# Grouping attention steps around column-tiled output products, with three more crossbar transposes, in a fused retention and feed-forward kernel

## Chip, cores, metric

One core of one Trainium2 chip. The metric is device microseconds of one execution; medians of several runs are quoted. A run over 1.5% above the fastest of its kernel counts as slow and is left out of ratios wherever enough fast runs are there. A ratio is the mean time of one kernel's fast runs over that of the other's of the same rounds, so it is not quite the ratio of the medians quoted beside it.

## The reference

```
q, k, v: (8, 8, 576, 64) float32        # batch, heads, sequence, head dim
gamma[h] = 1 - 2 ** (-5 - h)
scores   = (q @ k.T) / 8 * gamma ** (i - j) for i >= j, else 0
x = (scores @ v), heads side by side    # (4608 tokens, 512)
h = x @ w_in                            # (4608, 2048)
out = (h * sigmoid(beta * h)) @ w_out   # (4608, 512)
```

## The kernel before

The sequence is cut into chunks of 128 rows (the fifth of each batch has 64), 40 in all, and retention is linear: a chunk needs its own masked scores and a running state. Per chunk: prepare (scale queries, cast keys, scale values), transpose queries and keys, scores, mask, output = masked scores x values + queries x state, update the state. The result lands in `xT`, which feeds projections in blocks of 512 tokens: 16 `up` groups of four products, then 16 `down` groups of four. Attention of the next block is interleaved with the projections of this one: each step has a position counted in groups.

```python
NV = 3
vpads = [consts.tile([P, H, P], BF16, name=f"vpad{i}") for i in range(NV)]   # values, zero padded

def a_X(i):                     # transposes by DMA, issued from ScalarE
    ...
    nc.scalar.dma_start_transpose(qkT.rearrange("p j pr s -> p (j pr) s")[:, :, :cL],
                                  L["qk"][:cL].rearrange("p j h d -> p (j h d)"))

def a_sc(i):                    # scores: two heads side by side in half-row tiles
    ...
            nc.tensor.matmul(sc[j][:cL, p, :cL], L["kT"][r, p, :cL], L["qT"][r, p, :cL], ...)
    ...                         # two masks on VectorE

def a_O(i):
    ...
    if c > 0:                   # read the state
        for p in range(HP):
            nc.tensor.matmul(O[:, p, :cL], sbds[(i - 1) % NS][:, p, :], L["qT"][:, p, :cL], ...)
    for j in range(2):          # full-width products; the padding adds zeros for the other head
        for p in range(HP):
            nc.tensor.matmul(O[:, p, :cL], vp[:cL, 2 * p + j, :], R[:cL, j, p, :cL], ...)
    nc.vector.tensor_copy(xT[:, :, n0:n0 + cL], O[:, :, :cL])

def attn_steps(i, at, gap=2.0):
    if i < XB:                  # XB = 14: TensorE transposes
        return [(at - 4, F(pre, i)), (at - 3.9, F(load_next, i)), (at, F(a_T, i)), (at + gap, F(a_sc, i)),
                (at + 2 * gap, F(a_st, i)), (at + 2 * gap, F(a_O, i))]
    return [(at - 10, F(pre, i)), (at - 9.9, F(load_next, i)), (at - 5, F(a_X, i)), (at + gap, F(a_sc, i)),
            (at + 2 * gap, F(a_st, i)), (at + 2 * gap, F(a_O, i))]
```

So a crossbar transpose is issued at `at - 5` and its scores come at `at + 2`: seven groups of lead. A crossbar transpose is a DMA that transposes on its way; chunks before `XB` are transposed by TensorE instead. Lead is the distance from issue to use, latency the time from issue to landing.

## Time and profile before

| | before |
|---|---|
| time, median | 327.55 us (326.5 to 329.17) |
| span of the profiled run | 325.5 us |
| TensorE busy | 96% |
| first projection starts | 23.45 us |
| crossbar transposes | 26 |

In the lines of a profile PE is TensorE's products, PEld its weight loads, DVE is VectorE, ACT ScalarE (ACTq its queue, which issues DMAs), POOL GpSimd. A line of a timeline gives start and duration in us, engine, source line, operation, output<-inputs, shapes and count, and in brackets how long the engine had been idle and what ended that.

### The profile page before, as it was taken

What the parts mean: (1) busy time and instruction counts of PE and PEld (TensorE: products, weight loads), DVE (VectorE), ACT (ScalarE), POOL (GpSimd) and SP (SyncE); (2) the same over time, 40 slices, a digit from 0 to 9 for tenths busy, and PEclk for the clock granted to TensorE, in tenths of its full rate; (3) what the DMA queues carried; (4) which work ended last, traced back from release to release, by engine and by line L of the source; (5) the groups of instructions that cost most, each with busy time, mean ns of one, the idle gap of its engine ahead of it and who ended that gap; (6) DMA issues with size and microseconds to landing.
All of it is one profiled execution on the core that took longest, in us unless ns stands there. A gap on an engine that the chain in (4) does not pass through costs nothing.

```text
span 325.5 us, 5518 instructions
## 1 busy us (share of the span) xinstructions
PE 311.7 (96%) x2208; PEld 163.8 (50%) x2247; DVE 114.4 (35%) x202; ACT 141.6 (44%) x246; POOL 113.3 (35%) x132
## 2 busy tenths in 40 slices
PE   6779999999999999999999999999999999999995
PEld 2544584566555555544555555544545555544442
DVE  3685273634423244214423343224324432330011
ACT  2567881276237610760076106710662057305700
POOL 5323847974333354333333353333333430000000
PEclk9799999999999999999999999999999999999998
DMA  9999999999974999999999869656315121110011
GB/s 171 218 378 244 256 373 220 206 213 213 266 127 126 166 216 220 163 225 184 254 194 191 174 152 226 117 129 156 89 34 113 67 64 34 49 65 34 0 64 64
DMA packets 146362, 52.54 MB, mean 161 GB/s; under 512 B 137616, under 2 KB 137632, under 8 KB 146336
## 3 DMA queue, kind: packets, MB, share of 16 engines
q1 hardware_dynamic: 121920, 46.15, 63.8%
q10 hardware_dynamic: 24416, 6.04, 11.3%
q8 instruction: 17, 0.28, 0.4%
q14 instruction: 9, 0.07, 0.1%
HBM read 36.71 MB, written 9.44 MB: 142 GB/s over the span
## 4 chain that ended last, share of the span: by engine, by line
PE 91%; DVE 3%; DMA 2%; ACT 1%; issue 1%; ACTq 0%
PE po L296 38%; PE ph L284 37%; PE O L249 5%; PE sc L228 4%; PE st L266 2%; DMA qkT<-qk 2%; PE ph L152 2%; PE O L244 2%; PE T L212 2%; DVE R L232 1%; ACT qkT L216 1%; ACT sbd L272 0%; DVE xT L253 0%; DVE w_in_sb L130 0%; DVE tiny L160 0%
## 5 line engine op out<-in xcount | busy, mean ns | idle before, releaser
L284 PE MATMUL ph<-xT,w_in_sb 128*128 128x512 bf16 (+2 forms) x623 | 131.4, 357 | 2.5 <-DVE xT L253 1.6
L296 PE MATMUL po<-w_out_sb,gT 128*128 128x512 bf16 x556 | 130.2, 379 | 1.1 <-issue 0.2
L286 ACT ACTIVATE gT<-ph,beta_sb 128x512 bf16<-128x512 f32 (+2 forms) x160 | 101.9, 645 | 64.6 <-PE ph L284 48.2
L187 POOL TENSOR_TENSOR vpad<-qkvn,gv 128x512 bf16<-128x512 f32 (+1 forms) x40 | 42.0, 1051 | 135.9 <-issue 93.2
L284 PEld LDWEIGHTS <-w_in_sb 128*128 128x128 bf16 x640 | 59.1, 98 | 58.5 <-issue 1.6
L296 PEld LDWEIGHTS <-gT 128*128 128x128 bf16 x576 | 54.0, 98 | 60.6
L232 DVE TENSOR_TENSOR R<-sc,causal 128x512 bf16<-128x512 f32 (+1 forms) x80 | 47.2, 631 | 92.4 <-PE sc L228 92.2
L272 ACT CAST sbd<-st 64x256 bf16<-64x256 f32 x64 | 23.3, 364 | 77.2 <-PE st L266 76.4
L302 DVE COPY ot<-po 128x512 f32<-128x512 f32 x36 | 24.8, 691 | 66.1 <-PE po L296 63.9
L253 DVE CAST xT<-O 128x512 bf16<-128x512 f32 (+1 forms) x40 | 25.5, 637 | 38.2 <-PE O L249 38.2
L182 POOL TENSOR_TENSOR qk<-qkvn,gq 128x512 bf16<-128x512 f32 (+1 forms) x36 | 37.8, 1051 | 2.1 <-DMA qkvn<-in_q_dram 1.6
L249 PE MATMUL O<-R,vpad 128*128 128x128 bf16 (+1 forms) x320 | 23.5, 213 | 1.2 <-DVE R L232 1.2
L216 ACT COPY qkT<-T 128x1024 bf16<-128x1024 bf16 (+1 forms) x14 | 13.3, 950 | 21.8 <-PE T L212 21.7
L186 POOL CAST qk<-qkvn 128x512 bf16<-128x512 f32 (+1 forms) x36 | 21.9, 608 | 1.1 <-DMA qkvn<-in_k_dram 1.1
L249 PEld LDWEIGHTS <-vpad 128*128 128x128 bf16 (+1 forms) x320 | 18.2, 97 | 2.3 <-issue 1.8
L228 PEld LDWEIGHTS <-qkT 64*128 64x128 bf16 (+1 forms) x320 | 8.9, 98 | 17.7 <-issue 11.4
L228 PE MATMUL sc<-qkT 64*128 64x128 bf16 (+1 forms) x320 | 15.4, 217 | 0.9 <-ACT qkT L216 0.4
L266 PEld LDWEIGHTS <-qk 128*128 128x128 bf16 x128 | 9.5, 99 | 6.6 <-issue 0.2
L266 PE MATMUL st<-vpad,qk 128*128 128x128 bf16 x128 | 12.6, 222 | 0.1
L212 PE MATMUL T<-ident,qk 128*128 128x128 bf16 (+1 forms) x112 | 8.7, 224 | 3.1 <-DVE qk L182 3.0
L244 PE MATMUL O<-qkT,sbd 128*128 128x128 bf16 (+1 forms) x128 | 11.5, 212 | 0.0
L212 PEld LDWEIGHTS <-qk 128*128 128x128 bf16 (+1 forms) x112 | 7.2, 103 | 5.1 <-DVE qk L182 3.1
(38 smaller groups left out, 59.1 us busy)
## 6 DMA issues: line engine op xcount, KB each, us to landing
out_dram<-ot SPq DMA_DIRECT2D x36, 256.0 KB, 2.4
qkvn<-in_q_dram SPq DMA_DIRECT2D x32, 256.0 KB, 4.7
qkvn<-in_k_dram SPq DMA_DIRECT2D x32, 256.0 KB, 5.0
qkvn<-in_v_dram SPq DMA_DIRECT2D x32, 256.0 KB, 5.3
wt<-in_moe_w_in_dram SPq DMA_DIRECT2D x4, 1024.0 KB, 10.4
wt<-in_moe_w_out_dram SPq DMA_DIRECT2D x4, 1024.0 KB, 10.6
qkvn<-in_q_dram SPq DMA_DIRECT2D x8, 128.0 KB, 4.7
qkvn<-in_k_dram SPq DMA_DIRECT2D x8, 128.0 KB, 4.3
```

The costliest lines, as they stand in the source:

```text
L182: (nc.vector if first else nc.gpsimd).tensor_tensor(qn[:cL], t[:cL, 0], gq_b, ALU.mult)
L187: nc.gpsimd.tensor_tensor(vp4[:cL], t[:cL, 2].rearrange("p (pr two) d -> p pr two d", two=2), gv_b.rearrange("p (pr two) d -> p pr two d", ...
L228: nc.tensor.matmul(sc[j][:cL, p, :cL], L["kT"][r, p, :cL], L["qT"][r, p, :cL], start=True, stop=True, skip_group_check=True)
L232: nc.vector.tensor_tensor(R[:cL, j, :, :cL], sc[j][:cL, :, :cL], m_b, ALU.mult)
L249: nc.tensor.matmul(O[:, p, :cL], vp[:cL, 2 * p + j, :], R[:cL, j, p, :cL], start=(n == 0), stop=(j == 1), skip_group_check=True)
L253: nc.vector.tensor_copy(xT[:, :, n0:n0 + cL], O[:, :, :cL])
L266: nc.tensor.matmul(st[:, p, :], L["kn"][:cL, 2 * p:2 * p + 2, :].rearrange("p h d -> p (h d)"), L["vp4"][:cL, p], start=(c == 0 and p == 0 ...
L272: nc.scalar.copy(sbd[r, :, j * D:(j + 1) * D], st[r, :, j * D:(j + 1) * D])
L284: nc.tensor.matmul(ph[:, :tn], w_in_sb[:, ko, fo * P:(fo + 1) * P], xT[:, ko, x0:x0 + tn], start=(ko == 0), stop=(ko == KO - 1))
L286: nc.scalar.activation(gT[:, fo, t0:t0 + tn], ph[:, :tn], ACT.Silu, scale=beta_sb[:, fo:fo + 1])
L296: nc.tensor.matmul(po[:], gT[:, fo, ms * P:(ms + 1) * P], w_out_sb[:, fo, :], start=(fo == 0), stop=(fo == FO - 1))
L302: nc.vector.tensor_copy(ot, po[:])
```

## The change

The intent: spend less TensorE time per chunk by column tiles (two heads' outputs side by side), by visiting the attention less often (scores of chunk i with output and state of chunk i-1, in one cluster), and by leaving three more chunks' transposes to the crossbar; and start the projections earlier. Cut to its core:

```diff
-    XB = 14
+    XB = 11
-    NV = 3
-    vpads = [consts.tile([P, H, P], BF16, name=f"vpad{i}") for i in range(NV)]
+        vn = sb.tile([P, H, D], BF16, name="vn", tag="vn", bufs=4)
...
 def a_O(i):
-        if c > 0:  (state read first, then padded products)
+        for j, p in [(n // HP, n % HP) if i < 9 else (n % 2, n // 2) for n in range(H)]:
+            nc.tensor.matmul(O[j * D:(j + 1) * D, p, :cL], vn[:cL, 2 * p + j, :], R[:cL, j, p, :cL],
+                             start=(p == 0), stop=(c == 0), skip_group_check=True)
+        (then the state read, if c > 0)
...
+    def cluster(i, at):                       # chunks 9 and up
+            if i < XB:
+                st += [(at - 7, F(pre, i)), (at - 6.9, F(load_next, i)), (at - 3, F(a_T, i))]
+            else:
+                st += [(at - 10, F(pre, i)), (at - 9.9, F(load_next, i)), (at - 5, F(a_X, i))]
+            st += [(at, F(a_sc, i))]
+        if C0 <= i - 1 <= last:
+            st += [(at, F(a_O, i - 1)), (at, F(a_st, i - 1))]
...
 first stage, chunks 0 to 3
-    warm_up(12); betas(); pre(0); a_T(0); ...   (a_T(i + 1) ahead of a_O(i); key cast on ScalarE)
+    warm_up(3)  (float32); pre(0)
+    for i in range(4):
+        a_T(i)        # queries first, copied by ScalarE; keys copied by VectorE
+        warm_up(1, 256)
+        a_sc(i); pre(i + 1); a_st(i); a_O(i)     # key cast on VectorE
+    first quarter of w_in loaded and cast in two pieces of 256 columns
```

The transposes stay at `at - 5`, but the scores moved from `at + 2` to `at`.

More of the change, by code (lines that the diff above doesn't have):

```diff
@@ L72 @@
     nc.scalar.dma_start(beta_rows[:], moe_beta.rearrange("(fo p) -> fo p", p=P))
-    warm = consts.tile([P, MB], BF16, name="warm")
+    warm = consts.tile([P, MB], F32, name="warm")
     nc.vector.memset(warm[:], 0.0)
@@ L97 @@
                             fill=0.0, base=0, channel_multiplier=-1)
-    NV = 3
-    vpads = [consts.tile([P, H, P], BF16, name=f"vpad{i}") for i in range(NV)]
     NS = 2
     sbds = [consts.tile([P, HP, P], BF16, name=f"sbd{i}") for i in range(NS)]
-    nc.gpsimd.memset(vpads[0][:], 0.0)
     nc.vector.memset(sbds[0][:], 0.0)
-    nc.gpsimd.memset(vpads[1][:], 0.0)
     nc.vector.memset(sbds[1][:], 0.0)
@@ L115 @@
     WG = 4
-    FG = d_ff // WG
+    pieces = [(0, 256), (256, 256)] + [(f, 512) for f in range(512, d_ff, 512)]
+    NP = len(pieces)
     w_in_r = moe_w_in.rearrange("(ko ki) f -> ki ko f", ki=P)
     w_out_r = moe_w_out.rearrange("(fo fi) n -> fi fo n", fi=P)
-    wts = {}
+    wts, whole = {}, [None]
     def load_w_in(g):
-        t = stage.tile([P, KO, FG], F32, name="wt", tag="wt", bufs=4)
-        nc.sync.dma_start(t[:], w_in_r[:, :, g * FG:(g + 1) * FG])
+        f0, fn = pieces[g]
+        if f0 % 512 == 0:
+            t = stage.tile([P, KO, 512], F32, name="wt", tag="wt", bufs=4)
+            whole[0] = t
+        t = whole[0][:, :, f0 % 512:f0 % 512 + fn]
+        nc.sync.dma_start(t, w_in_r[:, :, f0:f0 + fn])
         wts[g] = t
@@ L127, in cast_w_in @@
         t = wts.pop(g)
+        f0, fn = pieces[g]
         for ko in range(KO):
             e = nc.gpsimd if ko == KO - 1 else nc.vector
-            e.tensor_copy(w_in_sb[:, ko, g * FG:(g + 1) * FG], t[:, ko])
+            e.tensor_copy(w_in_sb[:, ko, f0:f0 + fn], t[:, ko])
     def load_w_out(g):
@@ L134, in load_w_out @@
         nc.sync.dma_start(t[:], w_out_r[:, g * KO:(g + 1) * KO, :])
-        wts[WG + g] = t
+        wts[NP + g] = t
     def cast_w_out(g):
-        t = wts.pop(WG + g)
+        t = wts.pop(NP + g)
         for i in range(KO):
@@ L142, in cast_w_out @@
             e.tensor_scalar(w_out_sb[:, fo, :], t[:, i], rbeta_sb[:, fo:fo + 1], None, ALU.mult)
-    for g in range(WG):
+    for g in range(NP):
         load_w_in(g)
@@ L147, with warm_up @@
         load_chunk(b, c)
-    def warm_up(n):
+    def warm_up(n, cols=MB):
         ph = psum.tile([P, MB], F32, name="ph", tag="mm", bufs=3)
         for _ in range(n):
-            nc.tensor.matmul(ph[:], warm[:, :P], warm[:], start=True, stop=True, skip_group_check=True)
+            nc.tensor.matmul(ph[:, :cols], warm[:, :P], warm[:, :cols], start=True, stop=True,
+                             skip_group_check=True)
     def betas():
-        pb = psum.tile([P, FO], F32, name="pb", tag="T", bufs=1)
+        pb = psum.tile([P, FO], F32, name="pb", tag="mm", bufs=3)
         nc.tensor.transpose(pb[:], beta_rows[:], ident_f[:FO, :FO])
@@ L176, in pre @@
         qn, kn = qk[:, 0], qk[:, 1]
-        vp = vpads[i % NV]
-        vp4 = vp.rearrange("p (pr two) (x d) -> p pr (two x) d", two=2, x=2)[:, :, 0::3, :]
+        vn = sb.tile([P, H, D], BF16, name="vn", tag="vn", bufs=4)
         gq_b = gq[:cL, c, :].unsqueeze(2).to_broadcast([cL, H, D])
@@ L182, in pre @@
         (nc.vector if first else nc.gpsimd).tensor_tensor(qn[:cL], t[:cL, 0], gq_b, ALU.mult)
-        if first:
-            nc.scalar.copy(kn[:cL], t[:cL, 1])
-        else:
-            nc.gpsimd.tensor_copy(kn[:cL], t[:cL, 1])
-        nc.gpsimd.tensor_tensor(vp4[:cL], t[:cL, 2].rearrange("p (pr two) d -> p pr two d", two=2),
-                                gv_b.rearrange("p (pr two) d -> p pr two d", two=2), ALU.mult)
-        live[i] = dict(qk=qk, qn=qn, kn=kn, vp=vp, vp4=vp4)
+        (nc.vector if first else nc.gpsimd).tensor_copy(kn[:cL], t[:cL, 1])
+        nc.gpsimd.tensor_tensor(vn[:cL], t[:cL, 2], gv_b, ALU.mult)
+        live[i] = dict(qk=qk, qn=qn, kn=kn, vn=vn)
     def load_next(i):
@@ L209, in a_T @@
         T = psum.tile([P, 2, HP, P], BF16, name="T", tag="T", bufs=1)
-        for j, src in enumerate((L["qn"], L["kn"])):
+        T2 = psum.tile([P, 2, HP, P], BF16, name="T2", tag="mm", bufs=3) if i < 4 else T
+        qkT = sb.tile([P, 2, HP, P], BF16, name="qkT", tag="qkT", bufs=4)
+        for j, (src, t) in enumerate(((L["qn"], T), (L["kn"], T2))):
             for p in range(HP):
-                nc.tensor.transpose(T[:, j, p, :cL],
+                nc.tensor.transpose(t[:, j, p, :cL],
                                     src[:cL, 2 * p:2 * p + 2, :].rearrange("p h d -> p (h d)"),
                                     ident[:cL, :cL])
-        qkT = sb.tile([P, 2, HP, P], BF16, name="qkT", tag="qkT", bufs=4)
-        nc.scalar.copy(qkT[:, :, :, :cL], T[:, :, :, :cL])
+            if i < 4:
+                (nc.vector.tensor_copy if j else nc.scalar.copy)(qkT[:, j, :, :cL], t[:, j, :, :cL])
+        if i >= 4:
+            nc.scalar.copy(qkT[:, :, :, :cL], T[:, :, :, :cL])
         L["qT"], L["kT"] = qkT[:, 0], qkT[:, 1]
@@ L238, in a_O @@
         L = live[i]
-        R, vp = L["R"], L["vp"]
+        R, vn = L["R"], L["vn"]
         O = psum.tile([P, HP, P], F32, name="O", tag="O", bufs=1)
-        n = 0
+        for j, p in [(n // HP, n % HP) if i < 9 else (n % 2, n // 2) for n in range(H)]:
+            nc.tensor.matmul(O[j * D:(j + 1) * D, p, :cL], vn[:cL, 2 * p + j, :], R[:cL, j, p, :cL],
+                             start=(p == 0), stop=(c == 0), skip_group_check=True)
         if c > 0:
@@ L244, in a_O @@
                 nc.tensor.matmul(O[:, p, :cL], sbds[(i - 1) % NS][:, p, :], L["qT"][:, p, :cL],
-                                 start=(n == 0), stop=False, skip_group_check=True)
-                n += 1
-        for j in range(2):
-            for p in range(HP):
-                nc.tensor.matmul(O[:, p, :cL], vp[:cL, 2 * p + j, :], R[:cL, j, p, :cL],
-                                 start=(n == 0), stop=(j == 1), skip_group_check=True)
-                n += 1
-        n0 = b * S + c0
-        nc.vector.tensor_copy(xT[:, :, n0:n0 + cL], O[:, :, :cL])
-        del live[i]
+                                 start=False, stop=True, skip_group_check=True)
+        n0 = b * S + c0
+        if i == 3:
+            nc.vector.tensor_copy(xT[:, :2, n0:n0 + cL], O[:, :2, :cL])
+            nc.scalar.copy(xT[:, 2:, n0:n0 + cL], O[:, 2:, :cL])
+        else:
+            (nc.scalar.copy if i < 3 else nc.vector.tensor_copy)(xT[:, :, n0:n0 + cL], O[:, :, :cL])
     def a_st(i):
@@ L266, in a_st @@
             nc.tensor.matmul(st[:, p, :], L["kn"][:cL, 2 * p:2 * p + 2, :].rearrange("p h d -> p (h d)"),
-                             L["vp4"][:cL, p], start=(c == 0 and p == 0), stop=True,
+                             L["vn"][:cL, 2 * p:2 * p + 2, :].rearrange("p h d -> p (h d)"), start=(c == 0 and p == 0), stop=True,
                              skip_group_check=True)
@@ L320, in attn_steps @@
     def attn_steps(i, at, gap=2.0):
-        if i < XB:
-            return [(at - 4, F(pre, i)), (at - 3.9, F(load_next, i)), (at, F(a_T, i)), (at + gap, F(a_sc, i)),
-                    (at + 2 * gap, F(a_st, i)), (at + 2 * gap, F(a_O, i))]
-        return [(at - 10, F(pre, i)), (at - 9.9, F(load_next, i)), (at - 5, F(a_X, i)), (at + gap, F(a_sc, i)),
+        return [(at - 4, F(pre, i)), (at - 3.9, F(load_next, i)), (at, F(a_T, i)), (at + gap, F(a_sc, i)),
                 (at + 2 * gap, F(a_st, i)), (at + 2 * gap, F(a_O, i))]
-    warm_up(12)
-    betas()
+    warm_up(3)
     pre(0)
-    a_T(0)
-    nc.gpsimd.memset(vpads[2][:], 0.0)
-    pre(1)
     for i in range(4):
-        warm_up(2)
+        a_T(i)
+        warm_up(1, 256)
         a_sc(i)
+        if i < 3:
+            pre(i + 1)
         a_st(i)
+        a_O(i)
+        if i == 0:
+            betas()
         if i < 3:
-            a_T(i + 1)
-            if i < 2:
-                pre(i + 2)
-        else:
-            cast_w_in(0)
-            warm_up(2)
-        a_O(i)
+            warm_up(1, 256)
+    cast_w_in(0)
+    cast_w_in(1)
     fill = [F(up, 0, fo) for fo in range(FO)]
-    merged(fill, [(2, F(cast_w_in, 1)), (5, F(cast_w_in, 2)), (9, F(cast_w_in, 3))],
+    merged(fill, [(2, F(cast_w_in, 2)), (5, F(cast_w_in, 3)), (9, F(cast_w_in, 4))],
            [(5.1 + g / 10, F(load_w_out, g)) for g in range(2)],
@@ L372 @@
                                           if b * S + chunks[c][0] + chunks[c][1] >= (m + 1) * MB), len(order)))
-    todo = list(range(done, need(2)))
-    streams += [attn_steps(i, n1 + n * 30 / len(todo)) for n, i in enumerate(todo)]
-    done = need(2)
-    for m in range(2, NMB):
-        base = len(fill)
+    C0 = done
+    XB = 11
+    def cluster(i, at):
+        last = len(order) - 1
+        st = []
+        if i <= last:
+            if i < XB:
+                st += [(at - 7, F(pre, i)), (at - 6.9, F(load_next, i)), (at - 3, F(a_T, i))]
+            else:
+                st += [(at - 10, F(pre, i)), (at - 9.9, F(load_next, i)), (at - 5, F(a_X, i))]
+            st += [(at, F(a_sc, i))]
+        if C0 <= i - 1 <= last:
+            st += [(at, F(a_O, i - 1)), (at, F(a_st, i - 1))]
+        return st
+    for m in range(1, NMB - 1):
+        base = n1 if m == 1 else len(fill)
+        if m > 1:
+            fill += [F(up, m, fo) for fo in range(FO)]
+            fill += [F(down, m, ms, f0) for ms in range(MB // P) for f0 in range(0, FO, 4)]
+        todo = list(range(done, need(m + 1) + 1))
+        streams += [cluster(i, base + n * 31 / len(todo)) for n, i in enumerate(todo)]
+        done = need(m + 1) + 1
+    for m in range(NMB - 1, NMB):
         fill += [F(up, m, fo) for fo in range(FO)]
         fill += [F(down, m, ms, f0) for ms in range(MB // P) for f0 in range(0, FO, 4)]
-        if m + 1 < NMB:
-            todo = list(range(done, need(m + 1)))
-            streams += [attn_steps(i, base + n * 31 / len(todo)) for n, i in enumerate(todo)]
-            done = need(m + 1)
     merged(fill, *streams)
```

## The prediction

> **What bounds the kernel now.** I read the page first (busy shares, the chain of work that ended last), then TensorE's timeline in one stretch of the long middle, then the last stage, where no attention is left, and then what precedes the first projection.
>
> ```profile
> PE 311.7 (96%) x2208; PEld 163.8 (50%) x2247; DVE 114.4 (35%) x202; ACT 141.6 (44%) x246; POOL 113.3 (35%) x132
> ...
> PE 91%; DVE 3%; DMA 2%; ACT 1%; issue 1%; ACTq 0%
> ```
>
> TensorE is busy 96% of 325.5 us and carries 91% of the chain that ended last; no other engine passes 44%. So in the middle the end moves only by what is taken from TensorE's own stream, or by a new wait in it. Busy times overlap, so I cost by the distance from one group's start to the next group's start:
>
> ```profile
> 95.14 0.61 PE L212 MATMUL T<-ident,qk 128*128 128x128 bf16 x8
> 95.58 1.89 PE L284 MATMUL ph<-xT,w_in_sb 128*128 128x512 bf16 x8
> 97.41 0.40 PE L228 MATMUL sc<-qkT 64*128 64x128 bf16 x8
> 97.73 1.69 PE L284 MATMUL ph<-xT,w_in_sb 128*128 128x512 bf16 x7
> 99.47 0.39 PE L266 MATMUL st<-vpad,qk 128*128 128x128 bf16 x4
> 99.70 0.39 PE L244 MATMUL O<-qkT,sbd 128*128 128x128 bf16 x4
> 99.92 0.61 PE L249 MATMUL O<-R,vpad 128*128 128x128 bf16 x8
> 100.37 4.48 PE L284 MATMUL ph<-xT,w_in_sb 128*128 128x512 bf16 x20
> 104.78 0.31 PE L228 MATMUL sc<-qkT 64*64 64x64 bf16 x8
> ...
> 294.06 13.98 PE L284 MATMUL ph<-xT,w_in_sb 128*128 128x512 bf16 x63
> 307.87 13.98 PE L296 MATMUL po<-w_out_sb,gT 128*128 128x512 bf16 x63
> ```
>
> The last two lines: 64 products (one record is missing) take 307.87 - 294.06 = 13.81 us, 0.216 each. The program has 1152 such, so 249 us of 325.5 are projections that the change leaves alone. Of a chunk of attention: transposes 0.44 (95.14 to 95.58), state 0.23, state read 0.22, output through the zero-padded values 0.45 (eight at 0.056). The scores use half the rows each, in pairs that run side by side: four pairs at 0.056 would be 0.22, but 97.41 to 97.73 is 0.32, and the 20 projections before the scores at 104.78 take 4.41 where 20 x 0.216 = 4.32. So entering and leaving the scores costs some 0.095 us each; a group of full-array products costs no such step (99.47 - 97.73 = 1.74 = 8 x 0.216 + 0.01).
>
> The start:
>
> ```profile
> 20.50 1.29 DVE L232 TENSOR_TENSOR R<-sc,causal 128x512 bf16<-128x512 f32 x2 [0.22 <-PE sc L228]
> ...
> 21.71 1.09 DVE L130 CAST w_in_sb<-wt 128x512 bf16<-128x512 f32 x3
> ...
> 22.71 0.68 DVE L253 CAST xT<-O 128x512 bf16<-128x512 f32 x1
> ...
> 23.45 2.75 PE L284 MATMUL ph<-xT,w_in_sb 128*128 128x512 bf16 x12 [1.22 <-DVE xT L253]
> ```
>
> The first projection waits for VectorE's copy of the fourth chunk, itself behind three weight casts. ScalarE, VectorE and arriving loads, not TensorE, set these 23.45 us.
>
> **What the Trainium skill says.** "TensorEngine Tiling (Array Packing)", Key Properties: tiles work independently, and changing the tiling mode drains the array. The trace agrees on both: score pairs advance 0.056 us per pair, and each change of mode costs 0.095. The same page, Restrictions: column tiling switches fast weight load off. The trace has no column tile, but the short chunk's scores load 64-column weights, and all eight, with their entry and exit, take only 105.02 - 104.78 = 0.24 us; so I do not expect that to bind. "TensorE: Matmul & The Clock Gate", Part 1: idling drops the clock to half. The page's granted-clock row agrees: it reads 7 in the second slice (8 to 16 us), after TensorE idled 3.0 us waiting for the first queries. "SBUF — State Buffer" says that certain VectorE and GpSimd operations exclude each other on a shared port; the trace is consistent: w_in casts take 0.36 us each while GpSimd is idle (1.09 for three) and 0.50 while it casts (1.51 for three).
>
> **The change part by part.**
>
> *Column-tiled output.* From chunk 9 the eight output products alternate between two column halves. If pairs overlap as the scores' pairs do, 0.45 becomes 4 x 0.056 = 0.22. But grouping scores, output, state read and state passes through half-row, half-column, full: three mode changes per cluster, where the two insertions before had two (into and out of the scores). Per full chunk 0.45 - 0.22 - 0.095 = about 0.12 us off (0.01 of it the small step after the scores). 24 full chunks from chunk 9 on: 2.9 us. The 64-row chunks had four mode changes (scores and output each in and out) and eight products of 0.029; now three, and four pairs of about 0.03: 0.1 + 0.095 = 0.2 each, 7 of them: 1.4 us.
>
> *Chunks 4 to 8* get column tiles without alternation and without grouping: no overlap, and for the four full ones two more mode changes: 4 x 0.19 = 0.8 us lost.
>
> *Crossbar transposes from chunk 11, not 14*: three TensorE transposes fewer, 3 x 0.44 = 1.3 us.
>
> Middle, without new waits: 2.9 + 1.4 + 1.3 - 0.8 = 4.8 us. The built order confirms the groups: scores, output, state read, state in one place, 20 to 32 projections between clusters.
>
> *First stage.* Off TensorE: zero padding, ten warm-up products on net (the rest in float32, so longer), and the beta work ahead of the first queries. Chunk 0 can start when its loads and the warm-up allow, near 6.6 us by my count, instead of 9.71. But the interleaving changes: before, a chunk's transposes ran ahead of the previous output, and score masks started at 12.47, 15.22, 17.83, 20.50, 2.7 us apart. Now VectorE does per chunk, in series, two masks 1.29, query scaling 0.68, key cast 0.36 (ScalarE did that before), and half of the transposed copy, which I estimate at 0.5; with the TensorE steps between (0.4 after the cast, 0.45 before the masks) about 3.65 us. From masks of chunk 0 at about 8.2 plus 0.7 for beta: 8.2 + 0.7 + 3 x 3.65 = 19.9 for chunk 3, then 1.3 masks, 0.45 output, 0.65 split copy and 0.25 first cast of 256 columns: 22.5. Allowing for GpSimd's 1.04 us value scaling holding up casts, 23. So the gain is about 0.5 us, anywhere from -1 to +2. It is small because chunks no longer overlap.
>
> **The rivals.**
>
> *A wait for the crossbar replaces the transposes saved.* From issue to the scores were seven projection groups, 7 x 0.86 = 6.0, plus an attention group of 0.9. Now five groups and no attention between: about 4.3 us while up-projections run. What transposes take:
>
> ```profile
> DMA to landing us min/median/max: 2.6/3.2/7.1
> ```
>
> One of 6.8 us already held TensorE up by 0.39. Nine of 26 took over 4.4 us, all before 210 us, while loads were in flight. Chunk 11 is worst: its five groups are 320 columns wide, 5 x 0.55 = 2.75 us, in a stretch where the DMA row is 9 throughout. It may wait 1 to 3 us, more than the 0.44 its transposes cost. Against: in the down-projection ScalarE is free and issues early, and four value buffers instead of three move the loads to another moment. I put 2 us of waits into the centre; zero gives 322, 6 us gives 328.
>
> *Column pairs do not overlap*, because full-height weights or lost fast loading serialize them: then the 24 chunks lose 0.1 each instead of gaining 0.12, and the middle falls from 4.8 to about -1: 327 to 329. The overlap of the score pairs speaks against.
>
> *The first stage is limited by arrivals anyway, or the clock drops again.* The fourth chunk's values were scaled from 17.39 us on and w_in pieces of 1 MB landed 20.0, 24.0, 26.7 and 30.3 us in. Starting 2 us earlier, the fifth up-group would meet the second megabyte at about 24.5 with its cast; a start at 20.5 would be worth only 2 us. If short gaps throttle TensorE again, 1 us is lost.
>
> **The range.** 4.8 from the middle, 0.5 from the start, 0.4 from the old crossbar wait, less 2.0 of new waits: 3.7 us; 327.55 - 3.7 = 323.9. The change regroups with care, and probably keeps waits low, so I settle slightly lower, at 323.4. The best case (no waits, start gains 2) is 320; the worst inside the range, 6 us of waits, 327.5. Faster by over 2% needs below 321.0, almost the whole best case: 0.22. Slower by over 2% needs above 334, both rivals together: 0.04.
>
> **What would show it.** Right: alternating output groups (chunk 9 on) about 0.22 to 0.3 us to the next group's start; a first projection between 22 and 24 us; fewer than 90 TensorE transposes; still over 95% PE. Wrong: scores waiting for the transpose DMA for over 4 us in all; alternating output groups at 0.4 or more; projections slower than 0.216 each; a first projection before 21 us, which would mean that VectorE's series is shorter than I add up.

## More of the kernel before

The experiments ran in four jobs on three chips, each with the kernel before beside it (medians 326.7 to 327.9 us there); across jobs the ratios compare better than the times.

The prediction shows the main lines. Three more matter later: two rows of the page's 40 slices (8.1 us each; granted TensorE clock and DMA busy share in tenths), and from the view of waits the only wait of the scores for a transpose that TensorE felt (total us, times, longest).

```profile
PEclk9799999999999999999999999999999999999998
DMA  9999999999974999999999869656315121110011
```

```profile
PE sc L228 <- DMA qkT<-qk: 0.4, 1, 0.4
```

The clock drops once during the work, in the start (the last digit is the end of the run). The DMA engines are nearly full until some 190 us, but for a dip around 100 us: that is the traffic that transposes meet.

## The result

| | before | after |
|---|---|---|
| time, median | 327.08 us | 344.31 us (342.86 to 345.61) |
| ratio of fast runs | 1 | 1.051 (1.045 to 1.058) |
| span of the profiled run | 325.5 us | 342.7 us |
| first projection starts | 23.45 us | 21.96 us |
| first 320-column `up` group starts | 66.5 us | 67.7 us |
| last block's `up` starts | 294.1 us | 311.0 us |

Slower by 5%, where 1% faster was forecast. Up to 67 us the two kernels are within 1.2 us, and from the last block's `up` to the end it is 31.5 and 31.7 us; the time is lost in between: 227.5 us before, 243.3 us after. The page after, first the busy shares and then the two rows of slices:

```profile
PE 316.4 (92%) x2221; PEld 159.9 (47%) x2221; DVE 111.6 (33%) x210; ACT 135.8 (40%) x243; POOL 110.7 (32%) x130
...
PEclk9999999998999898999999899999999999999999
DMA  9999999997669988998998979954522231011011
```

TensorE idles 8% of the time, and the clock dips four times between 79 and 196 us. Waits after (us in total, times, longest), weight loads first, then the products:

```profile
PEld L229 <- DMA qkT<-qk: 20.8, 14, 3.3
PE sc L229 <- DMA qkT<-qk: 13.5, 10, 2.9
```

The same wait was 0.4 us once. (The view puts 0.75 us before the scores of chunk 14 down to VectorE, but that chunk's transposes landed at 101.01 us and its scores started at 101.05, so this is most likely one more such wait.) The view of the transposed tile says how long the transposes took:

```profile
DMA to landing us min/median/max: 2.7/4.3/7.8
```

Chunk 11, the first of the added transposes, shows one whole event. ScalarE's timeline has its issue, TensorE's timeline what follows:

```profile
73.57 1.53 ACTq L197 DMA_TRANSPOSE qkT<-qk  x1
```

```profile
75.73 1.25 PE L285 MATMUL ph<-xT,w_in_sb 128*128 128x320 bf16 x8 [0.65 <-ACT gT L287]
79.92 0.61 PE L229 MATMUL sc<-qkT 64*128 64x128 bf16 x8 [2.95 <-DMA qkT<-qk]
80.46 0.64 PE L244 MATMUL O<-R,vn 128*64 128x128 bf16 x8
81.03 0.61 PE L267 MATMUL st<-vn,qk 128*128 128x128 bf16 x4
```

Issued at 73.57, landed 6.3 us later at 79.88; the scores start at 79.92 after 2.95 us of idle. Two more things show. Before that, TensorE waited 0.65 us for ScalarE, whose queue the issue (1.53 us) had held up. And the scores then take 0.54 us to the next group instead of 0.32: the clock has halved. The table of stretches (PE, PEld, DVE, ACT, POOL busy us and instructions; granted clock; DMA share; GB/s) around it:

```profile
72.80:76.20 3.40, 2.75 (x24) 1.85 (x21) 1.30 (x3) 1.57 (x4) 2.62 (x3) 1.00 1.34 212
76.20:79.60 3.40, 0.78 (x6) 0.33 (x4) 0.00 (x0) 1.32 (x3) 1.04 (x1) 1.00 1.30 181
79.60:83.00 3.40, 3.08 (x26) 2.05 (x27) 1.89 (x3) 0.99 (x3) 1.22 (x2) 0.51 0.62 100
```

A stretch with TensorE busy 0.78 of 3.40 us is followed by 3.4 us at half clock, although TensorE is now busy. Later windows at 117.2, 134.3 and 192.3 us read 0.50 in the same way, just after or around the ends of waits of 2.44, 2.72 and 2.30 us; in the 3.41 us before each of these three TensorE was busy 1.0 to 1.1 us.

Where no load is in flight any more, the cluster is what was designed (TensorE's timeline after, late):

```profile
253.70 0.40 PE L229 MATMUL sc<-qkT 64*128 64x128 bf16 x8
254.02 0.41 PE L244 MATMUL O<-R,vn 128*64 128x128 bf16 x8
254.37 0.40 PE L248 MATMUL O<-qkT,sbd 128*128 128x128 bf16 x4
254.60 0.39 PE L267 MATMUL st<-vn,qk 128*128 128x128 bf16 x4
254.83 5.34 PE L285 MATMUL ph<-xT,w_in_sb 128*128 128x512 bf16 x24
```

From output to state read 0.35 us: four pairs of 0.056 plus one mode change of 0.12 (the step from one tiling of the array, here half columns, to another), against 0.45 for eight padded products.

### The profile page after: what moved, and what is told of

Its sections match the earlier page's. It is cut to its first block, busy times and chain, and to the rows that moved or that the text cites. A ratio compares the mean times of both kernels' runs of the same rounds, so it can differ in the third digit from the quotient of the medians.

```text
span 342.7 us, 5521 instructions
## 1 busy us (share of the span) xinstructions
PE 316.4 (92%) x2221; PEld 159.9 (47%) x2221; DVE 111.6 (33%) x210; ACT 135.8 (40%) x243; POOL 110.7 (32%) x130
## 3 DMA queue, kind: packets, MB, share of 16 engines
q10 hardware_dynamic: 27584, 6.83, 13.9%
## 5 line engine op out<-in xcount | busy, mean ns | idle before, releaser
L287 ACT ACTIVATE gT<-ph,beta_sb 128x512 bf16<-128x512 f32 (+2 forms) x160 | 99.3, 644 | 52.5 <-PE ph L285 48.0
L285 PEld LDWEIGHTS <-w_in_sb 128*128 128x128 bf16 x640 | 61.4, 99 | 63.3 <-issue 4.7
L184 POOL TENSOR_TENSOR vn<-qkvn,gv 128x512 bf16<-128x512 f32 (+1 forms) x40 | 41.6, 1041 | 38.8 <-DMA qkvn<-in_v_dram 13.0
L229 PE MATMUL sc<-qkT 64*128 64x128 bf16 (+1 forms) x320 | 15.9, 221 | 14.5 <-DMA qkT<-qk 13.5
L255 DVE CAST xT<-O 128x512 bf16<-128x512 f32 (+1 forms) x36 | 22.5, 625 | 5.2 <-PE O L248 4.7
L244 PE MATMUL O<-R,vn 128*64 128x128 bf16 (+1 forms) x320 | 18.6, 225 | 3.5 <-DVE R L233 3.5
L244 PEld LDWEIGHTS <-vn 128*64 128x64 bf16 (+1 forms) x320 | 11.8, 112 | 9.0 <-issue 5.7
L267 PE MATMUL st<-vn,qk 128*128 128x128 bf16 x128 | 13.1, 228 | 0.6 <-POOL vn L184 0.6
L153 PE MATMUL ph<-warm 128*128 128x256 f32 (+1 forms) x20 | 9.0, 552 | 1.5 <-DVE warm L75 1.5
L217 ACT COPY qkT<-T 128x1024 bf16<-128x1024 bf16 (+1 forms) x7 | 6.2, 889 | 9.5 <-PE T L211 9.5
L143 POOL TENSOR_SCALAR w_out_sb<-wt,rbeta_sb 128x512 bf16<-128x512 f32 x4 | 7.4, 1839 | 3.8 <-DMA wt<-in_moe_w_out_dram 3.8
```

The costliest lines, as they stand in the source:

```text
L184: nc.gpsimd.tensor_tensor(vn[:cL], t[:cL, 2], gv_b, ALU.mult)
L244: nc.tensor.matmul(O[j * D:(j + 1) * D, p, :cL], vn[:cL, 2 * p + j, :], R[:cL, j, p, :cL], start=(p == 0), stop=(c == 0), skip_group_check ...
L255: (nc.scalar.copy if i < 3 else nc.vector.tensor_copy)(xT[:, :, n0:n0 + cL], O[:, :, :cL])
L267: nc.tensor.matmul(st[:, p, :], L["kn"][:cL, 2 * p:2 * p + 2, :].rearrange("p h d -> p (h d)"), L["vn"][:cL, 2 * p:2 * p + 2, :].rearrange ...
L285: nc.tensor.matmul(ph[:, :tn], w_in_sb[:, ko, fo * P:(fo + 1) * P], xT[:, ko, x0:x0 + tn], start=(ko == 0), stop=(ko == KO - 1))
L287: nc.scalar.activation(gT[:, fo, t0:t0 + tn], ph[:, :tn], ACT.Silu, scale=beta_sb[:, fo:fo + 1])
```

## The experiments

Theory L: the crossbar transposes are issued too late for the latency that they have beside the loads; column tiles and grouping are sound. Rivals: C, the change moved the loads onto the transposes (four value buffers), and more lead would not help; G, grouping or column tiles slow TensorE.

**Eight groups of lead instead of five (a1_lead8).**

```diff
-    st += [(at - 10, F(pre, i)), (at - 9.9, F(load_next, i)), (at - 5, F(a_X, i))]
+    st += [(at - 13, F(pre, i)), (at - 12.9, F(load_next, i)), (at - 8, F(a_X, i))]
```

> The changed kernel with one edit: each crossbar transpose is issued eight projection groups ahead of its scores, not five (query and key preparation thirteen ahead, not ten). Theory L (the lead is too short): five groups give 4.1 to 4.7 us in the up stretches, eight groups with a cluster between give about 8 us, above every latency seen (7.75 us the longest), so TensorE waits for transposes fall from 13.5 us to under 2 us, the four half-clock windows go, and the time is about 322 to 325 us. Rival C (the transposes are slow because of the traffic they meet, and would be late wherever they are put): waits over 5 us stay and the time stays above 332 us.

324.18 us, ratio to before 0.987 (0.981 to 0.993): this one edit takes back 20 us and makes the kernel faster than before. Its waits, its clock row, and its transposes:

```profile
PE sc L229 <- DMA qkT<-qk: 1.1, 2, 0.9
```

```profile
PEclk9999999999999999999999999999999999999999
```

```profile
DMA to landing us min/median/max: 2.7/5.2/8.8
```

The transposes are not faster, they are even slower (5.2 us median); they are only early enough. So L holds, and C fails in its second half: more lead did help. (This edit moves the preparation of queries and keys forward too; b1_late, below, moves the transposes alone.)

**Crossbar from chunk 14 on again (a2_xb14).** `XB = 11` becomes `XB = 14`.

> The changed kernel with crossbar transposes from chunk 14 on, as before, instead of 11. Theory L: this takes away the wait of chunk 11 (about 3.9 us) and the half-clock window after it (about 1.7 us), and puts back three TensorE transposes (1.3 us): about 340 us. If the three added transposes were the whole trouble, it would come back to 325 us.

336.75 us, ratio 1.025 (1.017 to 1.033): 7.6 us were given back where 4 were expected, but 12.5 us above a1_lead8 stay, with 11.5 us of waits. The three added transposes are not the main trouble; the ones that were there before now come late.

**No loads from chunk 16 on (a3_no_loads), a wrong result.**

```diff
 def load_chunk(b, c):
+    if order.index((b, c)) >= 16:
+        qkv_tiles[(b, c)] = kept[c]      # a chunk of the same place, still resident
+        return
```

> Wrong result on purpose: from chunk 16 on no query, key or value is loaded, chunks 10 to 14 stay in place and are used again, so transposes meet no loads. Both L and C: transpose latency falls to about 3.1 us, below the lead of 4.1, waits for them after chunk 14 under 1 us, no half clock from there, and about 325 to 329 us (chunk 11 still waits). Rival G (the grouping itself, or column tiles, slows TensorE): stays above 338 us.

329.49 us (two runs). One wait is left, 3.4 us of chunk 11 (its loads are still there); all later transposes land before they are needed, with the lead still at five groups:

```profile
PE sc L233 <- DMA qkT<-qk: 3.4, 1, 3.4
```

```profile
DMA to landing us min/median/max: 2.6/3.1/6.6
```

The 6.6 is chunk 11. So what the latencies had above 3.1 us came with the loads, and G fails: same clusters, 15 us less than the changed kernel.

**The kernel before with five groups of lead (b1_late).** `at - 5` of the transposes becomes `at - 3`, nothing else.

> The kernel before with one edit: its crossbar transposes are issued five projection groups ahead of the scores, not seven, which is the changed kernel's distance. Theory L: with the latencies of the kernel before (eight of the up-stretch ones over 4.3 us) TensorE waits 5 to 9 us for transposes, perhaps one or two half-clock windows, 333 to 338 us. Rival C (the trouble is the changed kernel's own load timing, from four value buffers): under 330 us.

335.44 us, ratio 1.023 (1.016 to 1.031), inside the expected band, without any part of the change (preparation stays where it was, so only the issue is later):

```profile
PE sc L228 <- DMA qkT<-qk: 7.3, 7, 1.8
```

**Filler in the long waits (e1_filler).** `warm_up(4 if i == 11 else 2)` before the scores of chunks 11, 16, 18, 25.

> The changed kernel with float32 warm-up products put right before the scores of chunks 11, 16, 18 and 25, which waited 2.4 to 3.9 us for their transposes and were each followed by a half-clock window: 3.4 us of products before chunk 11, 1.7 us before the others. They fill waiting time, so they cost little. Theory: the waits themselves throttle the clock, so the four half-clock windows go and the time falls by 5 to 7 us, to about 338 us, while the transposes land as late as before. If the half clock has another cause, it stays at 343 to 346 us.

346.01 us median, two of four runs slow; the fast ones, 343.1 and 343.8, give 1.051, the same as without filler. A miss. (The waits of TensorE's products at these four places were 2.30 to 2.95 us, not 2.4 to 3.9.) The mean granted clock of the fast runs was 1.00 and 0.995, against 0.98 to 0.985 in the changed kernel's: most of the half clock went, and the time stayed. The one profile is of a slow run, so it illustrates and decides nothing. In it the four half-clock windows are gone, one dip of double length (6.8 us) stands at chunk 24, and 12.8 us of waits are there besides the fillers' own 8.5 us (20 passes of 0.427):

```profile
PEclk9999999999999999999997899999999999999999
```

```profile
PE sc L229 <- DMA qkT<-qk: 12.8, 10, 2.7
```

The clocks of the fast runs fit that the half clock comes from the waits, as does its absence in a1_lead8. What it costs by itself is not shown, since the fillers cost time of their own: in this profile those of chunks 11 and 25 ended 1.9 and 1.8 us after the transposes had landed. Nor does the length of a wait alone decide: 2.33 us at chunk 12 were followed by no dip here, 1.81 us in a2_xb14 were.

**No crossbar at all (e2_no_xbar).** `XB = 99`.

> The changed kernel with no crossbar transpose at all: all chunks are transposed on TensorE. No wait for transposes is left, and 29 chunks cost 23 x 0.447 + 6 x 0.34 = 12.3 us more on TensorE than in a1_lead8 (324.2): about 336 us. So doing without the crossbar should still beat the changed kernel (344.3) by 8 us. If grouping or column tiles were the trouble, it would be at 350 us or more.

335.23 us, ratio 1.027 (1.024 to 1.029). As expected: 9 us better than the changed kernel with no crossbar transpose, 11 us worse than with well-timed ones (12.3 expected). Here late transposes cost more than no crossbar.

**Three value buffers (e3_vn3).** `bufs=4` of the values becomes `bufs=3`.

> The changed kernel with three value buffers instead of four, as the padded ones were before; lead unchanged at five groups. If the fourth buffer moves loads into the transposes' way (their latency in chunks 14 to 28 rose from a mean of 4.6 us before to 5.4 us), latencies go back to 4.6, waits to about 9 us and the time to 335 to 338 us. If not, it stays within 2 us of 344.

346.84 us median, with two of four runs slow. The recorded ratio, 1.064 (1.059 to 1.069), cannot be that of the two fast runs: 342.2 and 345.4 over the kernel before of this job (mean 326.9) give 1.052, against 1.051 for the changed kernel. Waits 13.2 us, mean latency of chunks 14 to 28 5.2 us. Nothing comes back, so the fourth buffer was not what lengthened the latencies.

**A try at a better version (e4_best): nine groups of lead, and repairs to the early chunks.**

```diff
+    state read first in chunks 1 to 8; alternation from chunk 7
-    [(4, F(cast_w_out, 0)), ...
+    [(4.5, F(cast_w_out, 0)), ...            # behind the masks of chunk 6
-    first = i < 4
+    first = i < 5                            # chunk 4 prepared on VectorE
-    (at - 8, F(a_X, i))   (of a1_lead8)
+    (at - 9, F(a_X, i))                      # preparation one or two groups earlier too
```

> Attempt at a version better than a1_lead8 (324.2 us): crossbar lead of nine groups; state read ahead of the column products in chunks 1 to 8, so that it runs while the masks are awaited (before had that order), alternation from chunk 7; first w_out cast behind the masks of chunk 6 on VectorE; queries and keys of chunk 4 prepared on VectorE. Estimated 1 + 1 + 0.5 + 0.5 us less: about 321 us. If those early waits are not on the path, it stays at 324 us.

323.95 us, ratio 0.991 (0.988 to 0.993), one of six runs slow: not clearly better than a1_lead8 (0.987, and 0.995 when repeated below). Of the 3 us expected from these edits together none shows; they were not tried one by one.

**The key cast of chunks 0 to 3 on ScalarE again (f2_key_act).**

```diff
-    (nc.vector if first else nc.gpsimd).tensor_copy(kn[:cL], t[:cL, 1])
+    (ScalarE copy for i < 4, else as e4_best)
```

> e4_best with the key cast of chunks 0 to 3 back on ScalarE, as before. VectorE's series per chunk gets 0.42 us shorter, and meets GpSimd's value scaling less (query scaling took 1.34 us instead of 0.68 where they met). If VectorE's series sets the start, the first projection begins near 22.5 us instead of 23.6, and the time is about 1 us below e4_best's 323.95. If not, no change.

323.78 us, ratio 0.986 (0.982 to 0.989), two of six runs slow: 0.2 us below e4_best in time, half a percent in the ratio, in another job on another chip, so a small gain is not excluded. The first projection starts at 21.69 us in its profile, but the first 320-column `up` group at 67.7 us, no earlier than in e4_best (67.3 us). An earlier first projection is given back within the first blocks.

**Column tiles alone (f3_cols_only): the kernel before, with tiled outputs from chunk 9.**

```diff
+    if i >= COL0:                            # COL0 = 9
+        for m in range(H):                   # state read first, as before
+            j, p = m % 2, m // 2
+            nc.tensor.matmul(O[j * D:(j + 1) * D, p, :cL], vp[:cL, 2 * p + j, :], R[:cL, j, p, :cL], ...)
```

> The kernel before with column-tiled output products from chunk 9 on as its only change: scores, state and output stay in their own places, seven groups of lead, crossbar from chunk 14. By the accounting of 0.1 us per mode change, the pairs save 0.45 - 0.22 and the two more changes cost 0.19 to 0.2 in full chunks; the seven short ones save 0.1 each: 1 to 2 us in all, 325 to 326 us, no wait for transposes beyond the old 0.4 us. If column tiles by themselves were slow, 329 us or more.

327.06 us, ratio 0.999 (0.996 to 1.002): about 0.5 us by the ratio, which cannot be told from nothing, and less than the 1 to 2 us expected. TensorE's timeline shows where it goes:

```profile
238.49 0.39 PE L278 MATMUL st<-vpad,qk 128*128 128x128 bf16 x4
238.72 0.39 PE L251 MATMUL O<-qkT,sbd 128*128 128x128 bf16 x4
239.03 0.41 PE L257 MATMUL O<-R,vpad 128*64 128x128 bf16 x8
239.38 0.82 PE L296 MATMUL ph<-xT,w_in_sb 128*128 128x512 bf16 x3
```

The outputs take 0.35 us instead of 0.45, but the state read before them takes 0.31 instead of 0.22: one mode change going in and one going out eat the 0.22 us that the pairs save.

**The old start with the new middle.** f1_old_start and f4_old_start_tuned put the first stage and chunks 0 to 8 of the kernel before ahead of the clusters with eight and nine groups of lead.

> The first stage and chunks 0 to 8 of the kernel before (zero-padded values), with the changed kernel's grouped column-tiled middle and the crossbar lead of eight groups, so a1_lead8 without the changed start. In seven of eight profiles of the changed first stage the first projection began at 23.6 to 24.3 us, not the 22.0 of the first profile, against 22.5 and 23.5 with the old one. If the changed start is worth nothing, this is 0.5 to 1.5 us faster than a1_lead8 (324.2), since chunks 5 to 8 also keep fewer mode changes (4 x 0.19): about 323. If the changed start is worth its 1.5 us, this is at 325 us or more.

> f1_old_start with a lead of nine groups and the first w_out cast behind the masks of chunk 6: about 1 to 1.5 us below f1_old_start, 321.5 to 322 us, the best version of this study if the accounting holds.

Both gave a wrong result (325.42 and 329.91 us): I kept dense values in the three padded buffers, and preparation 13 groups ahead overwrote them before they were read. Their times decide nothing. The mended one holds two dense buffers in each padded one:

```diff
-    vp = vpads[i % NV][:, :HP, :]...
+    vp = vpads[i % NV][:, (i // NV % 2) * HP:(i // NV % 2 + 1) * HP, :]...
```

> f1_old_start mended: f1's three value buffers were overwritten before they were read (wrong result); here each padded buffer holds two dense ones, six in all. First stage and chunks 0 to 8 as before, grouped column-tiled middle with eight groups of lead. If the changed first stage and its early chunks are worth nothing, this is as fast as the eight-group kernel run beside it, or 0.5 to 1.5 us faster; if they are worth the 1.5 us that the first profile showed, it is 1 us or more slower.

Its partner, a1_lead8 again on the same chip in the same rounds:

> a1_lead8 once more, as the partner of g1_old_start on the same chip and in the same rounds, and to narrow its interval: 323 to 325 us, 0.985 to 0.992 of before.

325.43 and 325.47 us, ratios 0.995 (0.992 to 0.998) and 0.995 (0.992 to 0.998). The changed first stage with its early chunks is worth nothing in either direction. (Here both profiles had a half-clock dip in the first projections, which the first a1_lead8 had not. In the two jobs together a1_lead8 gains between 0.5% and 1.3% over before.)

## Why the prediction was wrong

**The bound.** Right: TensorE's stream carries the end, and both what was taken from it and the waits put into it show in the time. With the waits PE fell to 92%; over 95% was named as a sign of being right.

**The middle.** Right. Taken from the first 320-column `up` group to the last block, a1_lead8 needs 222.7 us, before 227.5: 4.8 us less. Its scores of chunk 9 lie ahead of that stretch (0.33 us), and it waits 0.7 us more for transposes; without these two it gained 5.2 us, and 2.9 + 1.4 + 1.3 = 5.6 were predicted for these chunks. Per full chunk the cluster takes 254.83 - 253.70 + 0.10 = 1.23 us, against 0.32 + 0.10 + 0.23 + 0.22 + 0.45 + 0.01 = 1.33 before: 0.10 saved, 0.12 predicted. Mode changes of this size have to be paid: f3_cols_only, with tiles but no grouping, gained next to nothing.

**Rival: pairs do not overlap.** Did not happen: the alternating groups took 0.35 us, against 0.4 or more as the sign of being wrong. That was a little above the 0.22 to 0.3 named as right, because the mode change is in it. The weight loads of the tiles took 0.112 us on average, of the padded products before 0.097, and did not bind.

**Rival: the crossbar wait.** This is the step that failed, by its size. The mechanism was named, with the lead of "about 4.3 us", nine latencies above it and chunk 11 as the worst; the runs showed all three. But the sum took in "2 us of waits" and the rival's worst case was 6 us. Measured: 13.5 us, where over 4 us was the prediction's own sign of being wrong. And the figures to see it were on the table: of the transposes issued in an `up` stretch, those of chunks 16, 19, 20, 23, 25 and 28 took longer than 4.3 us, and (5.24 + 4.89 + 6.83 + 7.14 + 4.81 + 5.52) - 6 x 4.3 = 8.6 us (b1_late, which does just that, waited 7.3 us); I then discounted it with the hope that the change was tuned. Two more things raised it. The latencies themselves rose, from a mean of 4.6 us in chunks 14 to 28 to 5.4: without loads they are 3.1 (a3_no_loads), the fourth buffer is not the reason (e3_vn3), and which loads they met more often stays open. And the four longest waits were each followed by half clock; I had the throttle as a rival for the start only.

**What 20.6 us consist of.** Between the same two landmarks the changed kernel takes 243.3 us and a1_lead8 222.7. Of the difference 12.4 us are waits of products for transposes (13.5 - 1.1). The other 8.2 us coincide with the 0.75 us before the scores of chunk 14, the 0.65 us for ScalarE's held queue, and the four half-clock windows, which can cost up to 4 x 1.7 = 6.8 us: together just 8.2, so nothing large is left to place. They need not add up: in e1_filler filling the four longest waits won no time, though the clock rose, and why is not shown.

**The start.** A gain of about 0.5 us was predicted; over the whole kernel none shows (g1_old_start). The first projection came at 21.96 us in the profile after, better than the 23 predicted, but at 23.6 to 24.3 us in seven other profiles with that stage, and at 22.5 to 23.6 us in six with the old one. One difference between an early and a late one is the exclusion that the prediction named ("value scaling holding up casts"), though here it held up the query scaling. VectorE's and GpSimd's timelines in the profile after, then in a1_lead8:

```profile
12.51 0.68 DVE L182 TENSOR_TENSOR qk<-qkvn,gq 128x512 bf16<-128x512 f32 x1
```

```profile
13.84 1.04 POOL L184 TENSOR_TENSOR vn<-qkvn,gv 128x512 bf16<-128x512 f32 x1 [2.57 <-DMA qkvn<-in_v_dram]
```

```profile
13.98 1.34 DVE L182 TENSOR_TENSOR qk<-qkvn,gq 128x512 bf16<-128x512 f32 x1
```

```profile
13.74 1.04 POOL L184 TENSOR_TENSOR vn<-qkvn,gv 128x512 bf16<-128x512 f32 x1 [2.47 <-DMA qkvn<-in_v_dram]
```

GpSimd scales the values of chunk 2 at nearly the same time in both. Where VectorE is 1.5 us early it scales the queries first, in 0.68 us; where it comes just after GpSimd has begun, the same operation takes 1.34 us. The Trainium skill's "SBUF — State Buffer", Who interferes with whom, says that a VectorE instruction with two SBUF inputs contends with a GpSimd instruction that reads SBUF; these lines agree. Why VectorE came 1.5 us later was not traced. And even the early start was given back: in the changed kernel itself the first `down` began at 49.7 us, before at 48.7.

**The chances.** "Slower by over 2%" had 0.04, for "both rivals together". One rival, at more than twice the worst size that I allowed (13.5 against 6 us of waits) and with the half clock on top, was enough.

## What to carry to other kernels

When a step is handed to a DMA, compare the distance from issue to use with the whole distribution of its latencies under traffic, item by item, and put that sum into the centre, not into a rival: here 5 groups of lead cost 20 us, 8 cost none, and doing without the crossbar cost 11. Count the distance again whenever steps are regrouped, because moving the consumer forward shortens it without a line about the DMA changing. Count the mode changes too before using tiles: here column tiles alone gained next to nothing, and about 0.10 us a chunk when grouped with the other steps.

## What the Trainium skill lacked or had wrong

- "DMA: Bandwidth & Descriptors", DMA Transpose (X-bar), and its rules for kernel authors give constraints, and say: "A transpose next to ordinary DMAs needs nothing." That holds for the result, not for the time: with 256-byte-row loads in flight a transpose of 128x1024 bf16 took up to 8.8 us from issue to landing, 3.1 us (median) without. No latency of that kind is given for trn2.
- "TensorEngine Tiling (Array Packing)", Key Properties: the drain at a mode change has no figure. Here 0.09 to 0.12 us each, in the kernel before, the changed one and f3_cols_only.
- "TensorE: Matmul & The Clock Gate", Part 3, has weight loads overlap with running products only if the row group differs, though shortly before it allows a background weight buffer too. Here products on all rows started every 0.056 us while a weight load took about 0.10, so loads for the same rows did overlap (254.37 to 254.83 us in the lines above); column tiles, also on all rows, did so with loads of 0.11.
- The same page, Part 1, has the clock fall after an idle window of about 3.4 us. Here the windows before the four dips were not idle: TensorE was busy 0.7 to 1.1 of 3.41 us in them, and single waits of 2.30 to 2.95 us were enough.
